# Gate and value layers by seven block products, float64 weights split from bytes, Mish as one ScalarE function

## The chip, the cores and the metric

The kernel runs on one NeuronCore of a Trainium2 chip. The metric is the device time of one execution in microseconds (us). Before the change the median of 3 runs is 508.99 us (508.86 to 509.68). The engines are called PE (TensorE), ACT (ScalarE), DVE (VectorE), POOL (GpSimd) and SP (SyncE, which issues the DMAs). SBUF is the on-chip memory, PSUM the accumulator memory that PE writes to, in banks of 128 x 512 float32.

## What is computed

Inputs q, k, v are float32, of shape (2, 8, 576, 64); the five weight matrices are float64.

```python
def _attn_ref(q, k, v):
    # factor 4: means of 4 neighbours in q, k, v give a small full attention, repeated 4 times;
    # added to it: attention within |i - j| < 4
    return (out_up + out_local).astype(np.float32)

def _moe_ref(x, w_in, w_out):                     # 512 -> 2048 -> 512
    h = x @ w_in
    sp = np.where(h > 20.0, h, np.log1p(np.exp(np.minimum(h, 20.0))))
    g = h * np.tanh(sp)                           # Mish
    return (g @ w_out).astype(np.float32)

def _moe2_ref(x, w_gate, w_val, w_out):           # 512 -> 1536 -> 512
    g = x @ w_gate
    silu = g * (1.0 / (1.0 + np.exp(-g)))
    val = x @ w_val
    return (silu * val @ w_out).astype(np.float32)

def reference(**kwargs):
    attn_out = _attn_ref(q, k, v)                 # (2, 8, 576, 64) -> x: 1152 tokens x 512
    x = _moe_ref(x=x, w_in, w_out)
    return _moe2_ref(x=x, w_gate, w_val, w_out)
```

## The kernel before

All activations stand with features on the partitions and the 1152 tokens along the row, in three pieces of 384 tokens (`PIECES`). Every float32 operand of a large product is split into a high part, which the float32r type of PE holds, and the rest, a low part. One product is then three matmuls: high x high, high x low, low x high (`mm3`, lines 755 to 758).

There are five stages on PE. Attention runs first, with dummy matmuls (`warm`, line 1091) where the planner has nothing else. Layer 1 (`l1`) has 16 chunks f of 128 features; a chunk and a token piece are 4 products along the 512 inputs, 12 matmuls of 384 columns into one PSUM bank, called a group here. The first pieces of chunks 0 to 5 are done within attention. Layer 2 (`l2`) has 4 blocks of 4 chunks; per block 12 groups (4 output slices e by 3 pieces i), which are added up in `yacc` in SBUF; after the last block `yacc` is split into `yb`. Layer 3 (`l3`) has 12 chunks; per chunk and piece a gate group and a value group, both on `yb`. Layer 4 (`l4`) has 3 blocks of 4 chunks, each with 9 groups of 12 matmuls of 512 columns. The order is: attention, layer 1 chunks 0 to 7, layer 2 block 0, layer 1 chunks 8 to 11, block 1, chunks 12 to 15, blocks 2 and 3, layer 3 chunks 0 to 7, layer 4 block 0, layer 3 chunks 8 to 11, layer 4 blocks 1 and 2. PSUM has 7 banks for all of this (`bank`).

A layer 1 group is copied out of its bank to H (line 224 on ACT, 226 on DVE). When the three pieces of a chunk are there, `mish` computes h * tanh(softplus(h)) as h * sin(pi/2 - 2 * arctan(...)): Tanh (line 809), Arctan (812) and Sin (815) on ACT, two chunks at a time, since Tanh and the other two need different function tables and a change of table costs an ACT_TABLE_LOAD; then a multiplication (819), the high part (224 or 226) and the low part (825) on DVE. Layer 3 takes Silu out of PSUM (919), multiplies with the value bank (922) and splits (224, 930).

A weight chunk is 512 KB of float64 (`convert`). SP loads it as pairs of 32-bit words into one of three `raw` buffers. Then the float32 is put together in `cw`, 128 x 512: magnitude of the upper word (297 on ACT or 299 on DVE), clamp (303), shift (307), three bits from the lower word (312), sign (317), all on DVE; then the high part (224 or 226) and the low part (333) go to one of eight `wt` buffers. There are 68 chunks: 16 for layer 1, 16 for layer 2, 12 each for gate, value and layer 4.

The order on every engine is made before the program is built: `Plan.add` takes each operation with its engines, an estimated duration, what it depends on, buffers, a due time `want`, and a mark for the function table; `Plan.run` goes through time and gives each free engine the ready operation with the earliest due time. An operation whose table mark differs from the current one is put off by 8 us and charged 1.28 us (`TABLE`); an ACT operation without a mark is taken to need no table. The order is then fixed: engines run in order, and only semaphores delay them. The table loads themselves are put in when the program is compiled, wherever an ACT function is not in the table that is loaded.

## Time and profile before

| | before |
|---|---|
| median of 3 runs | 508.99 us (508.86 to 509.68) |
| profiled execution, span of the program on the core | 507.6 us |
| PE busy | 500.7 us (99%) |
| DVE busy | 383.9 us (76%) |
| ACT busy | 277.0 us (55%) |
| granted TensorE clock, mean | 0.999 of 2.4 GHz |
| DMA | 48.2 MB, 95 GB/s over the span |

The span runs from the first to the last instruction of the profiled execution; the runs are timed by themselves, and their median lies 1.4 us above that span. Busy times are shares of the whole span, over stages that differ: a view by stretches of time tells what an engine does in each. Matmuls are pipelined, so the length of one is longer than its share of PE's time. Idle time of an engine matters only where another waits for it.

### The profile page before, as it was taken

The page shows a single profiled execution, that of the slowest core. Times are in us where ns is not written, and L with a number is a line of the kernel's source. Part 1 is how long each engine was busy: PE and PEld are TensorE (multiplying, and loading weights), DVE is VectorE, ACT ScalarE, POOL GpSimd, SP SyncE. Part 2 cuts the span into 40 slices and gives each one's busy share as a digit, 9 for nine tenths or more (in the row PEclk, how much of TensorE's full clock was granted, in tenths as well). Part 3 has the DMA queues.
Part 4 walks back from the last instruction along what each step waited for, and adds up shares of the span by engine and source line. Part 5 has one row for each costly group of instructions (what it writes and reads, how often), then busy time and mean ns, then how long its engine had stood idle before and what let it go on. Part 6 is the DMA issues. An engine that isn't in the chain of part 4 may idle for free.

```text
span 507.6 us, 8722 instructions
## 1 busy us (share of the span) xinstructions
PE 500.7 (99%) x3387; PEld 469.4 (92%) x3387; DVE 383.9 (76%) x771; ACT 277.0 (55%) x579; POOL 23.8 (5%) x45
## 2 busy tenths in 40 slices
PE   9999999999999999999999999999999999999997
PEld 7777779999999999999999999999998899998885
DVE  3898999999989999999699996667763298622322
ACT  3889999599995695679243634443432443310000
POOL 4432220000000000000000000000000000000000
PEclk9999999999999999999999999999999999999999
DMA  9999533451213521261205253222222032000022
GB/s 175 198 167 219 145 87 114 128 167 41 85 41 125 165 85 46 79 209 41 84 1 166 74 167 93 83 85 84 83 84 83 1 124 85 0 1 0 1 94 92
DMA packets 58225, 48.23 MB, mean 95 GB/s; under 512 B 30664, under 2 KB 53448, under 8 KB 58184
## 3 DMA queue, kind: packets, MB, share of 16 engines
q1 hardware_dynamic: 58184, 47.68, 34.2%
q8 instruction: 26, 0.43, 0.4%
q14 instruction: 15, 0.12, 0.1%
HBM read 45.31 MB, written 2.36 MB: 94 GB/s over the span
## 4 chain that ended last, share of the span: by engine, by line
PE 92%; ACT 3%; DVE 3%; DMA 1%; issue 1%; SPq 0%; ACTq 0%
PE b L756 23%; PE b L757 23%; PE b L758 23%; PE b L952 5%; PE b L951 5%; PE b L950 5%; PE warm L1091 2%; PE b L691 1%; PE b L636 1%; PE b L676 1%; ACT ed L535 1%; PE b L456 1%; DMA vw<-in_v_dram 1%; ACT ex L650 1%; PE b L520 1%
## 5 line engine op out<-in xcount | busy, mean ns | idle before, releaser
L756 PE MATMUL b<-xy,wt 128*128 128x384 f32 x480 | 161.3, 336 | 0.0
L758 PE MATMUL b<-xy,wt 128*128 128x384 f32 x480 | 160.4, 334 | 0.0
L757 PE MATMUL b<-xy,wt 128*128 128x384 f32 x480 | 160.4, 334 | 0.0
L756 PEld LDWEIGHTS b<-xy,wt 128*128 128x128 f32 x480 | 90.1, 188 | 0.4
L757 PEld LDWEIGHTS b<-xy,wt 128*128 128x128 f32 x480 | 90.1, 188 | 0.0
L758 PEld LDWEIGHTS b<-xy,wt 128*128 128x128 f32 x480 | 90.1, 188 | 0.0
L757 PE MATMUL b<-G,wt 128*128 128x384 f32 x192 | 64.2, 335 | 0.0
L756 PE MATMUL b<-G,wt 128*128 128x384 f32 x192 | 64.1, 334 | 0.0
L758 PE MATMUL b<-G,wt 128*128 128x384 f32 x192 | 64.1, 334 | 0.0
L224 ACT ACTIVATE G<-H 128x384 fp32r<-128x384 f32 (+1 forms) x38 | 21.7, 575 | 65.5 <-DVE H L922 44.5
L297 ACT ACTIVATE cw<-raw 128x512 f32<-128x512 f32 x58 | 39.0, 675 | 31.2 <-DVE wt L333 19.4
L333 DVE TENSOR_TENSOR wt<-cw,wt 128x512 fp32r<-128x512 f32 x68 | 46.1, 685 | 1.5 <-ACT wt L224 0.3
L312 DVE SCALAR_TENSOR_TENSOR cw<-raw,cw 128x512 uint32<-128x512 uint32 x68 | 46.4, 688 | 0.5
L317 DVE SCALAR_TENSOR_TENSOR cw<-raw,cw 128x512 uint32<-128x512 uint32 x68 | 46.3, 686 | 0.3
L952 PE MATMUL b<-wt,G 128*128 128x512 f32 x108 | 42.1, 389 | 0.0
L951 PE MATMUL b<-wt,G 128*128 128x512 f32 x108 | 42.0, 389 | 0.0
L950 PE MATMUL b<-wt,G 128*128 128x512 f32 x108 | 42.0, 389 | 0.0
L224 ACT ACTIVATE wt<-cw 128x512 fp32r<-128x512 f32 x41 | 25.0, 627 | 26.5 <-PE b L757 23.1
L922 DVE TENSOR_TENSOR H<-b,H 128x384 f32<-128x384 f32 x36 | 19.9, 553 | 24.8 <-PE b L758 24.8
L965 DVE TENSOR_TENSOR acc<-b,acc 128x512 f32<-128x512 f32 x18 | 12.4, 692 | 34.6 <-PE b L952 34.6
L757 PEld LDWEIGHTS b<-G,wt 128*128 128x128 f32 x192 | 36.0, 188 | 0.3 <-DVE G L825 0.3
L758 PEld LDWEIGHTS b<-G,wt 128*128 128x128 f32 x192 | 36.0, 188 | 0.0
(90 smaller groups left out, 751.6 us busy)
## 6 DMA issues: line engine op xcount, KB each, us to landing
raw<-in_moe_w_out_dram SPq DMA_DIRECT2D x28, 512.0 KB
raw<-in_moe_w_in_dram SPq DMA_DIRECT2D x16, 512.0 KB
raw<-in_moe_w_gate_dram SPq DMA_DIRECT2D x12, 512.0 KB
raw<-in_moe_w_val_dram SPq DMA_DIRECT2D x12, 512.0 KB
vw<-in_v_dram SPq DMA_DIRECT2D x36, 70.0 KB
vq<-in_v_dram SPq DMA_DIRECT2D x8, 288.0 KB
out_dram<-acc SPq DMA_DIRECT2D x9, 256.0 KB
qk<-in_q_dram SPq DMA_DIRECT2D x8, 256.0 KB
```

The lines of the kernel that those rows point to most:

```text
L224: ACT.activation(out, in_, AF.Copy)
L297: ACT.activation(cw.tile, h.bitcast(F32), AF.Abs)
L312: DVE.scalar_tensor_tensor(out=c, in0=words()[:, :, 0], scalar=29, in1=c, op0=ALU.logical_shift_right, op1=ALU.bitwise_or)
L317: DVE.scalar_tensor_tensor(out=c, in0=words()[:, :, 1], scalar=0xC0000000, in1=c, op0=ALU.bitwise_and, op1=ALU.bitwise_or)
L333: DVE.tensor_tensor(out=wt.tile[:, 1], in0=cw.tile, in1=wt.tile[:, 0].bitcast(F32), op=ALU.subtract)
L756: PE.matmul(out=ps, lhsT=wt_hi, rhs=m_hi, start=first, stop=False)
L757: PE.matmul(out=ps, lhsT=wt_hi, rhs=m_lo, start=False, stop=False)
L758: PE.matmul(out=ps, lhsT=wt_lo, rhs=m_hi, start=False, stop=last)
L922: DVE.tensor_tensor(out=h.tile[:, cs], in0=pv.tile[:, 0:n], in1=h.tile[:, cs], op=ALU.mult)
L950: PE.matmul(out=ps.tile, lhsT=g[:, 0, tok], rhs=wt[:, 0], start=(f == fs[0]), stop=False)
L951: PE.matmul(out=ps.tile, lhsT=g[:, 0, tok], rhs=wt[:, 1], start=False, stop=False)
L952: PE.matmul(out=ps.tile, lhsT=g[:, 1, tok], rhs=wt[:, 0], start=False, stop=(f == fs[-1]))
```

## The change

Three things are done, and the planner's rules stay as they are.

**Weights.** `convert` loads the same 512 KB, as bytes, into a `raw` tile of 4104 bytes per partition, at byte 1. Seen as 32-bit words from byte 0, the upper word of each pair then holds the float64's bits shifted by a byte. Its sign and the top exponent bits are the byte at 8 (read as int8, every 8th). `fold` and `field` make the float32's upper bits from it on ACT, both with the function Prelu, without a table mark; `join` shifts the word right by 5 and puts both together on DVE. High and low part follow as before. `cw` has 3 buffers, not 4.

```diff
-            o = plan.add({"ACT": us_act(512), "DVE": us_ts(512)}, mag, [o_load, prev.get("mag")], w0, [cw], [raw])
-            o_mag = o
-            for fn, d in ((range_, us_ts(512)), (shift, us_ts(512)), (low, us_tt(512)), (sign, us_tt(512))):
-                o = plan.add({"DVE": d}, fn, [o], w0 + 1, use=[cw, raw])
+            def fold(e):
+                ACT.activation(cw.make(), raw.tile[:, 8:4104].bitcast(I8).rearrange("p (n b) -> p n b", b=8)[:, :, 0],
+                               AF.Prelu, scale=-1.0, bias=-56.0, alpha=SLOPE)
+
+            def field(e):
+                ACT.activation(cw.tile.bitcast(I32), cw.tile, AF.Prelu, scale=-2.0 ** 27 / SLOPE, bias=-112 * 2.0 ** 27, alpha=SLOPE)
+
+            def join(e):
+                DVE.scalar_tensor_tensor(out=cw.tile.bitcast(U32), in0=raw.tile[:, 0:4096].bitcast(U32).rearrange("p (n b) -> p n b", b=2)[:, :, 1],
+                                         scalar=5, in1=cw.tile.bitcast(U32), op0=ALU.logical_shift_right, op1=ALU.bitwise_or)
+
+            o_mag = o = plan.add({"ACT": us_act(512) + 0.1}, fold, [o_load, prev.get("mag")], w0, [cw], [raw])
+            o = plan.add({"ACT": us_act(512)}, field, [o], w0, use=[cw])
+            last = plan.add({"DVE": us_tt(512)}, join, [o], w0 + 1, use=[cw, raw])
```

**Mish.** Tanh, Arctan, Sin and the multiplication go. The first two pieces of chunks 0 to 5, done within attention, are copied to H and later passed through Mish in place, 768 columns at once; all other groups of layer 1 leave PSUM through Mish on ACT. Both carry the mark "mish". G has 6 buffers, not 7, and the T buffers go.

```diff
+            if early:
+                copy(e, h.tile[:, cs], ps.tile[:, 0:n])
+            else:
+                ACT.activation(h.tile[:, cs], ps.tile[:, 0:n], AF.Mish)
+        if early:
+            o = plan.add({"ACT": us_act(n, True), "DVE": us_tt(n)}, evac, [o], want - 4, use=[ps, h])
+        else:
+            o = plan.add({"ACT": us_act(n, True)}, evac, [o] + att_ops, want - 4, use=[ps, h], table="mish")
...
+        if f < RING:
+            h.ops.append(add({"ACT": us_act(n)}, mish, h.ops[:2] + att_ops, want - 2, use=[h], table="mish"))
+        o = add({"ACT": us_act(NTOK), "DVE": us_ts(NTOK)}, hi, h.ops + att_ops, want + 4.0, [g], [h])
```

**Seven products.** For the first two token pieces, layer 3 takes two chunks, the two halves of the 512 inputs and the two pieces as 2 x 2 blocks and computes them by seven block products (a Winograd form of Strassen's scheme) of 6 matmuls each, where eight products took 48. `combine` makes two sums and differences of weight halves per pair of chunks, each with its own high and low part; `turn_tokens` makes four differences of token blocks at the end of layer 2 (one in `yb`, three in new `tok` tiles). In `products` some sums run in PSUM: bank `pa` takes four products, and its state is copied to SBUF after the first, second and third of them before the next is added on; three sums are finished on DVE. The third piece goes on as before, in groups.

```diff
+        o1 = product(pa, (kind, f), 0, y(0, 0), raw[0], True, False, [yb], home)
+        k1 = keep(pa, hold.slots[0], [o1])
+        o2 = product(pb, (kind, f), 1, y(1, 0), raw[1], True, True, [yb])
+        c11 = add_(pb, hold.slots[0], [o2, k1])
+        o5 = product(pc, (kind, f, 0), 0, t[0], tok_ops[0:1], True, False, [yb])
+        o6 = product(pa, (kind, f, 0), 1, t[1], [tok_ops[1], k1], False, False, [tok[0]])
+        k2 = keep(pa, hold.slots[1], [o6])
+        o7 = product(pa, (kind, f, 1), 0, t[2], [tok_ops[2], k2], False, False, [tok[1]])
+        k3 = keep(pa, hold.slots[2], [o7])
+        c22 = add_(pc, hold.slots[2], [o5, k3])
+        o4 = product(pa, (kind, f + 1), 1, t[3], [tok_ops[3], k3], False, True, [tok[2]])
+        o3 = product(pc, (kind, f, 1), 1, y(1, 1), raw[2] + [c22], False, True, [yb])
+        c12 = add_(pc, hold.slots[1], [o3, k2])
...
+        todo = [(0, block(0, 1), block(0, 0), given[0, 1] + given[0, 0]), (1, block(1, 1), view(tmp[0]), given[1, 1]),
+                (2, block(1, 1), block(0, 1), given[1, 1] + given[0, 1]), (3, block(1, 0), view(tmp[1]), given[1, 0])]
...
+            o = plan.add({"DVE": us_tt(2 * PC)}, sub_, deps + more, want, [tmp[x]], [yacc] + ([tmp[0]] if x == 1 else [tmp[1]] if x == 3 else []))
+            subs.append(o)
+            o = plan.add({"ACT": us_act(2 * PC), "DVE": us_ts(2 * PC)}, hi, [o, yb.first], want, [tok[x - 1]] if x else [], [tmp[x]] + ([] if x else [yb]))
+            o = plan.add({"DVE": us_tt(2 * PC)}, lo, [o], want, use=[tmp[x], tok[x - 1] if x else yb])
...
+        a = plan.add({"DVE": us_tt(256)}, add_(0, 0, half(c1, 0), half(c1, 1), ALU.add), [o1, o0], w0, [s0], [c1])
+        b = plan.add({"DVE": us_tt(256)}, add_(1, 0, half(c0, 0), half(c1, 0), ALU.subtract), [o1, o0], w0, [s1], [c0, c1])
+        a = plan.add({"DVE": us_tt(256)}, add_(0, 1, half(s0, 0), half(c0, 0), ALU.subtract), [a], w0, use=[s0, c0])
+        b = plan.add({"DVE": us_tt(256)}, add_(1, 1, half(c0, 1), half(s0, 1), ALU.subtract), [a, b], w0, use=[s1, c0, s0])
```

The planner orders everything anew. Three places show how. First ACT, at chunks 2 to 4 of layer 1 in the kernel before (T is the buffer of the Mish steps, H a chunk's evacuated rows):

```order
L809 ACT_TABLE_LOAD
L809 ACTIVATE T0_1589<-H2_1286 128x1152
L297 ACTIVATE cw2_1077<-raw2_1023 128x512
L809 ACTIVATE T1_1611<-H3_1385 128x1152
L224 ACTIVATE H0_1027<-b6_241 128x384
L812 ACT_TABLE_LOAD
L812 ACTIVATE T0_1589<-T0_1589,half_83 128x1152
L815 ACT_TABLE_LOAD
L815 ACTIVATE T0_1589<-T0_1589,half_pi_82 128x1152
L812 ACTIVATE T1_1611<-T1_1611,half_83 128x1152
```

And on ACT at chunks 5 to 7 of layer 1 in the changed kernel (L286 is fold, L290 field, L803 Mish out of a bank, L822 Mish in place):

```order
L286 ACTIVATE cw1_979<-raw2_1006 128x512
L822 ACT_TABLE_LOAD
L822 ACTIVATE H5_1459<-H5_1459 128x768
L290 ACT_TABLE_LOAD
L290 ACTIVATE cw1_979<-cw1_979 128x512
L803 ACT_TABLE_LOAD
L803 ACTIVATE H5_1459<-b6_237 128x384
L286 ACT_TABLE_LOAD
L286 ACTIVATE cw2_1065<-raw1_897 128x512
L803 ACT_TABLE_LOAD
L803 ACTIVATE H1_1110<-b2_195 128x384
```

A table load stood before every second or third function of the old steps, with copies and conversions between that took none; now one stands at each turn between a conversion and a Mish. The built program has 25 table loads before and 58 after.

Next DVE where layer 2 ends and layer 3 begins, before (L879 adds a bank to acc, L895 is the low part of yb, L333 that of a weight chunk):

```order
L879 TENSOR_TENSOR acc0_1875<-b5_233,acc0_1875 128x384
L226 CAST xy0_84<-acc0_1875 128x384
L895 TENSOR_TENSOR xy0_84<-acc0_1875,xy0_84 128x384
L333 TENSOR_TENSOR wt4_1427<-cw3_1132,wt4_1427 128x512
L879 TENSOR_TENSOR acc0_1875<-b2_199,acc0_1875 128x384
L333 TENSOR_TENSOR wt6_1521<-cw1_986,wt6_1521 128x512
```

And the same place on DVE after (L873 adds a bank to acc, L892 is the low part of yb, L920 a token difference, L928 its low part):

```order
L873 TENSOR_TENSOR acc0_1847<-b6_237,acc0_1847 128x384
L920 TENSOR_TENSOR H0_983<-acc0_1847,H4_1333 128x768
L892 TENSOR_TENSOR xy0_82<-acc0_1847,xy0_82 128x384
L920 TENSOR_TENSOR H5_1459<-acc0_1847 128x768
L928 TENSOR_TENSOR tok00_2891<-H0_983,tok00_2891 128x768
L920 TENSOR_TENSOR H1_1110<-acc0_1847,H0_983 128x768
L928 TENSOR_TENSOR tok10_2904<-H5_1459,tok10_2904 128x768
L873 TENSOR_TENSOR acc0_1847<-b5_229,acc0_1847 128x384
L928 TENSOR_TENSOR tok20_2917<-H1_1110,tok20_2917 128x768
L892 TENSOR_TENSOR xy0_82<-acc0_1847,xy0_82 128x384
```

Between the last two sums of the middle tokens and the low parts of the last tokens' columns there are now the differences and their low parts.

## Rows read from the trace of the kernel before

**Rows 1.** The page: engines' busy time; the chain that ended last, by engine and line.

```profile
PE 500.7 (99%) x3387; PEld 469.4 (92%) x3387; DVE 383.9 (76%) x771; ACT 277.0 (55%) x579; POOL 23.8 (5%) x45
...
PE 92%; ACT 3%; DVE 3%; DMA 1%; issue 1%; SPq 0%; ACTq 0%
PE b L756 23%; PE b L757 23%; PE b L758 23%; PE b L952 5%; PE b L951 5%; PE b L950 5%; PE warm L1091 2%; PE b L691 1%; PE b L636 1%; PE b L676 1%; ACT ed L535 1%; PE b L456 1%; DMA vw<-in_v_dram 1%; ACT ex L650 1%; PE b L520 1%
```

**Rows 2.** Stretches: length; busy us (count) of PE, PEld, DVE, ACT, POOL; clock; DMA; GB/s.

```profile
0.00:40.00 40.00, 37.59 (x445) 28.98 (x445) 28.59 (x76) 27.93 (x105) 15.91 (x36) 1.00 1.01 183
37.00:92.80 55.80, 55.13 (x719) 45.02 (x715) 53.03 (x149) 49.39 (x201) 9.28 (x11) 1.00 0.55 134
92.80:126.00 33.20, 33.20 (x194) 33.20 (x192) 31.65 (x58) 29.07 (x34) 0.00 (x0) 1.00 0.37 123
...
92.80:229.20 136.40, 136.40 (x787) 136.10 (x786) 128.93 (x224) 107.37 (x125) 0.00 (x0) 1.00 0.34 108
280.00:380.00 100.00, 100.00 (x578) 100.00 (x578) 74.28 (x148) 40.52 (x73) 0.00 (x0) 1.00 0.31 95
```

**Rows 3.** What PE waited for, longest sum first: us, times, longest.

```profile
PE warm L1091 <- DVE wsrc L375: 1.2, 1, 1.2
PE b L559 <- ACT ed L548: 0.5, 1, 0.5
```

**Rows 4.** Groups by line and shape on ACT: busy us, mean ns, idle before.

```profile
L297 ACT ACTIVATE cw<-raw 128x512 f32<-128x512 f32 x58 | 39.0, 675 | 31.2 <-DVE wt L333 19.4 <-DMA raw<-in_moe_w_out_dram 7.3 <-DMA raw<-in_moe_w_in_dram 3.9
L224 ACT ACTIVATE wt<-cw 128x512 fp32r<-128x512 f32 x41 | 25.0, 627 | 26.5 <-PE b L757 23.1 <-DVE cw L317 2.9 <-PE b L758 0.4
...
L815 ACT ACTIVATE T<-T,half_pi 128x1152 f32<-128x1152 f32 x16 | 20.1, 1259 | 0.2
...
L809 ACT ACTIVATE T<-H 128x1152 f32<-128x1152 f32 x16 | 18.7, 1167 | 0.7 <-DVE H L819 0.5
...
L919 ACT ACTIVATE H<-b 128x384 f32<-128x384 f32 x36 | 17.6, 488 | 31.6 <-PE b L758 31.6
L224 ACT ACTIVATE H<-b 128x384 f32<-128x384 f32 x27 | 13.0, 482 | 3.4 <-PE b L758 3.2
...
L812 ACT ACT_TABLE_LOAD x8 | 10.3, 1283 | 0.1
...
L224 ACT ACTIVATE G<-H 128x1152 fp32r<-128x1152 f32 x3 | 3.5, 1158 | 0.2 <-DVE H L819 0.2
```

**Rows 5.** ACT in order of time, around a table load: start us, us, what.

```profile
110.21 0.66 ACT L297 ACTIVATE cw<-raw 128x512 f32<-128x512 f32 x1
110.78 1.25 ACT L815 ACTIVATE T<-T,half_pi 128x1152 f32<-128x1152 f32 x1
...
112.30 0.66 ACT L297 ACTIVATE cw<-raw 128x512 f32<-128x512 f32 x1
112.97 1.28 ACT L809 ACT_TABLE_LOAD   x1
114.27 1.17 ACT L809 ACTIVATE T<-H 128x1152 f32<-128x1152 f32 x1
```

**Rows 6.** Groups on PE: busy us, mean ns of one, idle before.

```profile
L756 PE MATMUL b<-xy,wt 128*128 128x384 f32 x480 | 161.3, 336 | 0.0
...
L1091 PE MATMUL warm<-wsrc 128*128 128x256 bf16 x103 | 16.5, 297 | 1.2 <-DVE wsrc L375 1.2
```

**Rows 7.** Groups on DVE, low parts of 1152 and of 384 columns.

```profile
L825 DVE TENSOR_TENSOR G<-H,G 128x1152 fp32r<-128x1152 f32 x16 | 21.6, 1349 | 0.0
...
L895 DVE TENSOR_TENSOR xy<-acc,xy 128x384 fp32r<-128x384 f32 x12 | 6.6, 551 | 0.6 <-ACT xy L224 0.6
```

**Rows 8.** The chain that ended last, in order of time: start us, us, what.

```profile
56.46 4.05 DMA vw<-in_v_dram
...
91.98 0.85 PE b L691 x24
```

More of the change, by code (lines that the diff above doesn't have):

```diff
@@ L284, in load @@
             else:
-                nc.sync.dma_start(out=raw.tile, in_=src[128 * f:128 * (f + 1), :])
+                nc.sync.dma_start(out=t, in_=src[128 * f:128 * (f + 1), :])
         prev = conv_chain[0] or {}
@@ L788, in l1 @@
         ps, o, cs = cols_group("1", f, i, lambda: xt, xd + [h.first], want, [x_buf] + ([] if first else [h]), [h] if first else [])
+        early = f < RING and i < 2
         def evac(e):
-            copy(e, h.tile[:, cs], ps.tile[:, 0:n])
-        o = plan.add({"ACT": us_act(n, True), "DVE": us_tt(n)}, evac, [o], want - 4, use=[ps, h])
+            if early:
[6 more added lines that the diff above has]
+            o = plan.add({"ACT": us_act(n, True)}, evac, [o] + att_ops, want - 4, use=[ps, h], table="mish")
         if first:
@@ L797, in l1, with split, mish, hi @@
         if i == 2:
-            mish(f, h, want)
-    tanhs = []
-    def mish(f, h, want):
+            split(f, h, want)
+    def split(f, h, want):
         add = plan.add
-        g = G[f] = buf("g", GSHAPE, F32R, "G", 7)
-        t = buf("g", [128, NTOK], F32, "T", 2)
-        def tanh(e):
-            ACT.activation(t.make(), h.tile, AF.Tanh, scale=0.5)
-        def atan(e):
-            ACT.activation(t.tile, t.tile, AF.Arctan, scale=-0.5, bias=half)
-        def sin(e):
-            ACT.activation(t.tile, t.tile, AF.Sin, scale=-2.0, bias=half_pi)
-        def mult(e):
+        g = G[f] = buf("g", GSHAPE, F32R, "G", 6)
+        n = 2 * PC
+        def mish(e):
+            ACT.activation(h.tile[:, 0:n], h.tile[:, 0:n], AF.Mish)
+        def hi(e):
             g.make()
-            DVE.tensor_tensor(out=h.tile, in0=h.tile, in1=t.tile, op=ALU.mult)
-        def hi(e):
             copy(e, g.tile[:, 0], h.tile)
@@ L886, in l2 @@
         if fs[-1] == FF1 - 1:
+            y_full[e_, i] = o
             begin = yb.first is None
+            if i == 1 and e_ < 2:
+                return
             def hi(e):
@@ new lines, in products, with product, fn, keep @@
+    def products(kind, f, want, home, hold):
+        n = PC
+        p0, p1, p2 = [slice(c0, c0 + n) for c0, n in PIECES]
+        pa, pb, pc = bank(), bank(), bank()
+        for x in ((kind, f), (kind, f + 1), (kind, f, 0), (kind, f, 1)):
+            assert x in wts
+        y = lambda r, c: lambda z, j: yb.tile[:, z, 2 * r + j, (p0, p1)[c]]
+        t = [lambda z, j: yb.tile[:, z, j, p1]] + [lambda z, j, x=x: tok[x].tile[:, z, j] for x in range(3)]
+        raw = {0: [y_ops[e_, 0] for e_ in (0, 1)], 1: [y_ops[e_, 0] for e_ in (2, 3)], 2: [y_ops[e_, 1] for e_ in (2, 3)]}
+        def product(ps, w, half, m, deps, first, last, use, new=()):
+            def fn(e):
+                if first:
+                    ps.make()
+                for x in new:
+                    x.make()
+                wt = wts[w].tile
+                for j in range(2):
+                    cs = slice(256 * half + 128 * j, 256 * half + 128 * j + 128)
+                    mm3(ps.tile[:, 0:n], wt[:, 0, cs], wt[:, 1, cs], m(0, j), m(1, j), first and j == 0, j == 1, skip_group_check=True)
+            return plan.add({E_PE: 6 * us_mm(n)}, fn, list(deps) + [wt_ops[w]], want, ([ps] if first else []) + list(new),
+                            ([] if first else [ps]) + [wts[w]] + list(use))
+        def keep(ps, d, deps, w=None):
+            def fn(e):
+                copy(e, d(), ps.tile[:, 0:n])
+            return plan.add({"ACT": us_act(n, True), "DVE": us_tt(n)}, fn, deps, want - 4, use=[ps, hold])
+        def add_(ps, d, deps):
+            def fn(e):
+                DVE.tensor_tensor(out=d(), in0=ps.tile[:, 0:n], in1=d(), op=ALU.add)
+            return plan.add({"DVE": us_tt(n)}, fn, deps, want - 4, use=[ps, hold])
+        o1 = product(pa, (kind, f), 0, y(0, 0), raw[0], True, False, [yb], home)
[11 more added lines that the diff above has]
+        c12 = add_(pc, hold.slots[1], [o3, k2])
+        return pa, o4, c11, c12, c22
@@ L1045, in add_l3 @@
     def add_l3(b):
-        for f in blk(b):
-            for i in range(3):
-                groups.append(([("g", f), ("v", f)] if i == 0 else (), 2, lambda t, f=f, i=i: l3(f, i, t)))
+        for f in blk(b)[::2]:
+            groups.append(([("g", f, 2), ("v", f, 2)], 11.0, lambda t, f=f: l3(f, t)))
     def add_l4(b):
```

209 lines of the change are left out of this document (119 added, 90 removed).

## The prediction

> **What bounds the kernel now.** The page comes first [rows 1]: PE is busy 99% of the span, and 92% of the chain that ended last is PE, almost all of it the three matmul lines of the four layers. The list of what PE waited for says how rigid that is [rows 3]: the longest sum is 1.2 us at the start, the next 0.5. The table by stretch [rows 2] shows two parts. Up to 92.8 us there is attention, where PE runs small matmuls and dummies, and DVE (53.0 of 55.8 us in its second part) and ACT (49.4) are nearly full as well. The last attention products end at 92.8 [rows 8]; from there PE has no gap. So after 92.8 a matmul less is time gained, and a wait added is time lost, at full price. Before it, a gain must beat three engines.
>
> The price of a 384-column matmul is the stretch 280 to 380: 578 in 100.0 us, 0.173 us each [rows 2]. The 336 ns of its group [rows 6] is its length in a pipeline and not its cost.
>
> **What the change takes from PE.** In the built order the matmuls on xy and on the new tok tiles are 1368 where there were 1440: 12 sets of products save 6 each. 72 x 0.173 = 12.5 us, all of it in the gate and value stage, where PE has no gap. Nothing else on PE changes: the dummies are 103 in both orders [rows 6], the second and fourth layers have the same counts.
>
> **What it does to ACT in the first two layers.** This decides. Per weight chunk ACT had one magnitude instruction (675 ns [rows 4]), and on 10 of 68 not even that. Now it has two, fold and field, both Prelu. Mish replaces Tanh, Arctan and Sin (16 times 1.17 to 1.26 us each) and does most evacuations. That alone would unload ACT. But the built order has 58 table loads where the old one had 25: one stands at almost every change between Prelu and Mish, 28 of them on the lines of fold and field. The planner, which lets a table count only for the marked functions (Exp, Mish, Silu), does not know of these and strews conversions between Mish instructions. 56 of the 58 stand in the first two layers. A load takes 1283 ns [rows 4], and the next instruction starts 20 ns after it, the load itself 10 ns after the instruction before [rows 5]: 1.3 us each, nothing hidden.
>
> The ACT instructions of that part, by rows 4: 56 loads 72; 25 folds and 25 fields at 0.65 (the rows of 675 and 627 ns), 33; 36 Mish out of PSUM at 0.48, 17; 6 Mish of 768 columns at 0.84 (between the rows of 512 and 1152 columns), 5; 13 copies of 1152 at 1.16, 15; 20 shorter copies, 10. Sum 152 us, where PE has 136.4 us of work in the same part and ACT had 107.4 [rows 2]. ACT becomes the bound.
>
> How much of it reaches PE goes by banks. A group of 12 matmuls (2.08 us) fills one of seven PSUM banks, and a group cannot start before the bank of the group seven places earlier is evacuated. I went through the two orders stage by stage, adding the row durations on ACT and 0.173 us per matmul on PE.
>
> Stage I, the last 18 groups of layer 1 that follow attention. ACT's first Mish load stands behind one evacuation and one fold, at about 95.2. From it to the last Mish of chunk 7 there are 23 loads (29.5), 15 conversions (9.8), 13 evacuations (6.3), 6 Mish of 768 (5.0), 4 copies of 1152 (4.6) and 3 of 512 (1.9): 57.1 us, to 152.3. The bank that its last instruction but one gives back, at 151.8, is wanted by the fifth group of the second layer's first block after chunk 7; 270 matmuls stand between 92.8 and that group, so PE would be there at 139.5. PE is 12.3 us late. No slack is left out: the seven banks are in this number (without them it would be some 20).
>
> Stage II, chunks 8 to 11. PE leaves the second layer's first block at 154.0 + 12.3 = 166.3, ACT has caught up by then (the block needs 12 short evacuations) and is free at 167.8. To the eighth Mish evacuation there are 15 loads (19.2), 12 conversions (7.8), 8 evacuations (3.9) and 4 copies (3.6): 34.5 us, to 202.3. The group that wants this bank stands 168 matmuls after 166.3, at 195.4. PE loses 6.9 us more.
>
> Stage III, chunks 12 to 15: 14 loads, 18 conversions, 12 evacuations and 5 copies, some 40 us, beside 50 us of PE, and the planner has put chunk 12's evacuations on ACT early. By the same count no bank is late. Sum: 19.2 us. The ends: half of it if conversions run into each other as in the timeline (the row at 110.21 starts the next after 0.57 us, not 0.66), a few loads pass while PE is behind, and ACT starts a microsecond earlier, 12 us; with each handover between fold and field costing another 0.1 us, 24 us.
>
> The Trainium skill, ScalarE: Activation LUTs, section What ACT_TABLE_LOAD costs, states 1283 ns for the load and another 1380 ns for a drain, 2.66 us per switch. The trace agrees with the first and not with the second (the 20 ns of rows 5). By the page the 56 loads would cost 77 us more.
>
> **DVE, and the turn into the gate stage.** DVE loses four of five conversion steps per chunk and gains one, and gains the half-chunk sums, the sums out of PSUM and the four token differences. Per pair of chunks in the gate stage that is about 20 us of DVE by starts, beside 132 matmuls, 22.9 us; DVE ran 31.7 of 33.2 in the old first layer without PE waiting [rows 2, 3], so I price that at nothing. At the turn it shows: after the last sum of the middle tokens DVE has four differences and three low parts of 768 columns (0.95 us, between the rows of 384 and 1152 [rows 7]), seven short ones and two of 512 before the low part of the last tokens' columns, some 14 us in all, while PE has 8.3 us of the second layer, then 4 of 6-matmul products, 12.5 us, until it wants that. 2.0 us, between 0 and 3.
>
> **Attention.** ACT gets about 10 instructions more up to 92.8 (+6.6 us, against 6.4 us of idle time in 37 to 92.8 [rows 2]); DVE is relieved by about as much. PE's dummies stay in the order, and its gaps there are 0.7 us, so almost nothing can be gained. The one new kind of transfer, into a tile one byte off, is not in the trace. From below: as before. From above: as slow as the stretch with mostly 256-byte packets, 183 GB/s [rows 2], 2.9 us for 512 KB where the stretch 280 to 380 (0.31 busy for 95 GB/s) gives 1.7; the layers need 85 GB/s, so nothing is late there, but a value load that PE already waited for behind such loads [rows 8] would be a microsecond or two later. I take +1.5 us for attention, between -0.7 and +5.
>
> **The sum.** Against the profiled execution: 507.6 - 12.5 + 19.2 + 2.0 + 1.5 = 517.8. The median of the runs, 508.99, is 1.4 above that span: **519.2 us**.
>
> **The rivals.**
> The loads do not hold PE up, the saving stays: 507.6 - 12.5 + 2.0 + 1.4 = 498.5. For it speaks that ACT has 29 us of idle time in the old part [rows 2] and loses the three old functions. Without the 56 loads ACT would have 80 us of work against 136, and nothing would wait. Against it stand the loads in the order and the 1283 ns. It decides if fewer than about 30 of them were to run. 8%. The Trainium skill, ScalarE: Activation LUTs, section Table sets: the hidden batching unit, says that cheap functions such as relu, copy, identity and abs are in every set as filler; read so as to cover Prelu, it would give this rival's time. The built order has no load at Copy, but has them at Prelu.
>
> The product sets hold PE, on top of the forecast. The third and fourth product onto one bank wait for a copy of what stands there, with 6 matmuls (1.04 us) between: the last matmul's end lies 0.16 us after the next one's start [rows 6], the copy takes 0.49 [rows 4], so 0.3 us are left with the handovers unpriced. If at each of the 24 places a conversion of 0.65 us stands before the copy, 0.36 x 24 = 8.6 us: 528. For it: ACT and DVE are full of conversions there. Against: ACT's order has the copies waiting for PE, often in pairs with nothing between. 14%.
>
> PE's waits of 2 to 5 us in stage I could also lower its granted clock, which was 1.00 of the higher level (2.4 GHz) throughout; no row shows such a wait, so it is left to the upper end of the range.
>
> The skewed loads are slow by a factor of 4 or more: 7 us per chunk where PE uses one in 6.2, and the kernel would follow the DMA, above 560. Against: the stretch at 183 GB/s is the slowest of those that keep the DMA engines busy. 4%.
>
> Each table load empties ACT for as long again as it takes: 56 x 1.28 = 72 us more in the part that already holds PE, 591. Against it stand the 20 ns of rows 5; 2%. The Trainium skill, in the section on ACT_TABLE_LOAD named above, states nearly this.
>
> That the products do not save what they say is excluded by the counted matmuls.
>
> **How the numbers follow.** The forecast has 72%. Its own spread: 12 to 24 for the loads, 0 to 3 at the turn, -0.7 to +5 in attention, so 508 to 526, most of it within 513 to 525. What a measurement can tell from no change is 0.2%, 1.0 us. Faster by more: the first rival and a sliver of the forecast, 10%. Within: 4%. Slower: 86%. The range 509 to 528 leaves out the first rival, the upper part of the second and the two large ones, about 2 in 10.
>
> **What would show it.** In the changed profile: 58 table loads of 1283 ns; ACT busy nearly without gap from 95 to 152; at the top of PE's waits the Mish evacuation line, some 19 us in pieces of 1 to 5 us, none after the third chunk block; the two gate stages, 528 and 264 matmuls, at 0.173 us. Wrong would be: PE without waits there (first rival), waits on the copies between products, or on value loads in attention.

## The result, and the profile after

The changed kernel takes **517.21 us** (median of 4 runs, 516.17 to 518.08) where the kernel before takes 509.34 beside it: 1.015 times as long (95% interval 1.0132 to 1.0168). The forecast was 519.2. Measured once more beside other kernels it took 516.64, 1.0155 times (1.0132 to 1.0177).

The page of the changed kernel answers to [rows 1]: the span, the engines, the chain that ended last.

```profile
span 515.2 us, 8535 instructions
...
PE 494.1 (96%) x3315; PEld 459.3 (89%) x3315; DVE 323.2 (63%) x624; ACT 339.0 (66%) x681; POOL 23.9 (5%) x43
...
PE 75%; ACT 19%; issue 3%; DVE 2%; DMA 1%; ACTq 0%
```

ACT, 3% of the chain before, is 19% of it now, and PE has idle time. What it waited for stands in the list that answers to [rows 3] (us in all, times, longest):

```profile
PE b L763 <- ACT H L803: 14.2, 8, 4.1
```

L803 is Mish out of a bank: PE waits for banks. Where, the table by stretch shows. Its boundaries are the end of attention, the ends of layer 2's blocks 0, 1 and 3, and the gate and fourth-layer stages; columns as in [rows 2].

```profile
93.20:167.60 74.40, 65.00 (x359) 62.86 (x356) 27.95 (x43) 65.62 (x82) 0.00 (x0) 0.98 0.26 84
167.60:224.30 56.70, 51.27 (x289) 49.98 (x288) 23.38 (x37) 44.42 (x54) 0.00 (x0) 1.00 0.25 75
224.30:299.60 75.30, 75.30 (x434) 75.30 (x433) 49.11 (x82) 50.47 (x68) 0.00 (x0) 1.00 0.23 70
299.60:391.40 91.80, 91.80 (x531) 91.80 (x530) 83.13 (x155) 60.13 (x108) 0.00 (x0) 1.00 0.34 104
391.40:416.10 24.70, 24.70 (x110) 20.27 (x110) 5.50 (x12) 7.37 (x11) 0.00 (x0) 1.00 0.14 43
416.10:462.00 45.90, 45.90 (x265) 45.90 (x264) 39.75 (x70) 30.62 (x57) 0.00 (x0) 1.00 0.30 92
```

PE is idle in the first two of these stretches only, 9.4 and 5.4 us. In the first, ACT is busy for 65.6 us, more than the 62.0 us that this stretch takes PE without waits (the fourth experiment shows that). The two gate stretches, the fourth and the last row, take 137.7 us; before, 576 and 288 matmuls took 149.8.

The groups on ACT that answer to [rows 4], table loads and the two new steps (busy us, mean ns, idle before):

```profile
L286 ACT ACTIVATE cw<-raw 128x512 f32<-128x512 int8 x68 | 45.7, 672 | 12.1 <-DVE wt L307 11.3 <-DMA raw<-in_moe_w_out_dram 0.5
L290 ACT ACTIVATE cw<-cw 128x512 int32<-128x512 f32 x68 | 43.0, 633 | 0.9
L803 ACT ACT_TABLE_LOAD x23 | 29.5, 1283 | 0.4
...
L286 ACT ACT_TABLE_LOAD x17 | 21.8, 1283 | 0.3
...
L290 ACT ACT_TABLE_LOAD x11 | 14.1, 1283 | 0.2
...
L822 ACT ACT_TABLE_LOAD x5 | 6.4, 1283 | 0.1
...
L480 ACT ACT_TABLE_LOAD x1 | 1.3, 1283 | 0.7 <-PEq L1215 0.7
L1004 ACT ACT_TABLE_LOAD x1 | 1.3, 1283 | 0.0
```

58 loads of 1283 ns, 56 of them at Mish (L803, L822) and Prelu (L286, L290). In the gate stage, where Silu (L1004) alternates with Prelu, there is one: those two share a table. The timeline of ACT ahead of the longest wait (start us, us, what):

```profile
139.21 1.28 ACT L822 ACT_TABLE_LOAD   x1
140.50 0.84 ACT L822 ACTIVATE H<-H 128x768 f32<-128x768 f32 x1
141.36 1.28 ACT L290 ACT_TABLE_LOAD   x1
142.66 0.63 ACT L290 ACTIVATE cw<-cw 128x512 int32<-128x512 f32 x1
143.30 1.28 ACT L803 ACT_TABLE_LOAD   x1
144.60 0.49 ACT L803 ACTIVATE H<-b 128x384 f32<-128x384 f32 x1
```

Three loads stand around two functions of useful work, without a gap; at 145.09 a bank comes free. PE has been waiting for it since 141.03, as its timeline shows:

```profile
140.69 0.34 PE L765 MATMUL b<-G,wt 128*128 128x384 f32 x1
145.14 0.69 PE L763 MATMUL b<-G,wt 128*128 128x384 f32 x1 [4.11 <-ACT H L803]
145.62 0.52 PE L764 MATMUL b<-G,wt 128*128 128x384 f32 x1
```

### The profile page after: what moved, and what is told of

Same layout as the page of the kernel before. It is cut to its first block, busy times and chain, and to the rows that moved or that the text cites. A ratio compares the mean times of both kernels' runs of the same rounds, so it can differ in the third digit from the quotient of the medians.

```text
span 515.2 us, 8535 instructions
## 1 busy us (share of the span) xinstructions
PE 494.1 (96%) x3315; PEld 459.3 (89%) x3315; DVE 323.2 (63%) x624; ACT 339.0 (66%) x681; POOL 23.9 (5%) x43
## 4 chain that ended last, share of the span: by engine, by line
PE 75%; ACT 19%; issue 3%; DVE 2%; DMA 1%; ACTq 0%
PE b L763 17%; PE b L765 17%; PE b L764 17%; PE b L1051 5%; PE b L1053 5%; PE b L1052 5%; ACT L803 3%; PE warm L1194 2%; ACT L290 2%; ACT cw L286 2%; ACT L286 2%; ACT H L803 2%; PE b L643 2%; ACT cw L290 1%; PE b L698 1%
## 5 line engine op out<-in xcount | busy, mean ns | idle before, releaser
L763 PE MATMUL b<-xy,wt 128*128 128x384 f32 x384 | 129.9, 338 | 3.7 <-ACT H L803 3.7
L765 PE MATMUL b<-xy,wt 128*128 128x384 f32 x384 | 128.6, 335 | 0.0
L764 PE MATMUL b<-xy,wt 128*128 128x384 f32 x384 | 128.6, 335 | 0.0
L293 DVE SCALAR_TENSOR_TENSOR cw<-raw,cw 128x512 uint32<-128x512 uint32 x68 | 46.6, 687 | 64.3 <-ACT cw L290 64.2
L763 PE MATMUL b<-G,wt 128*128 128x384 f32 x192 | 66.2, 345 | 11.1 <-ACT H L803 10.5
L763 PEld LDWEIGHTS b<-xy,wt 128*128 128x128 f32 x384 | 72.1, 188 | 5.3 <-ACT H L803 4.7
L764 PEld LDWEIGHTS b<-xy,wt 128*128 128x128 f32 x384 | 72.1, 188 | 0.0
L765 PEld LDWEIGHTS b<-xy,wt 128*128 128x128 f32 x384 | 72.1, 188 | 0.0
L765 PE MATMUL b<-G,wt 128*128 128x384 f32 x192 | 65.1, 339 | 0.0
L764 PE MATMUL b<-G,wt 128*128 128x384 f32 x192 | 65.0, 338 | 0.0
L286 ACT ACTIVATE cw<-raw 128x512 f32<-128x512 int8 x68 | 45.7, 672 | 12.1 <-DVE wt L307 11.3
L219 ACT ACTIVATE G<-H 128x1152 fp32r<-128x1152 f32 x20 | 22.9, 1164 | 45.8 <-PE b L765 23.5
L763 PEld LDWEIGHTS b<-G,wt 128*128 128x128 f32 x192 | 36.5, 190 | 13.6 <-ACT H L803 12.8
L290 ACT ACTIVATE cw<-cw 128x512 int32<-128x512 f32 x68 | 43.0, 633 | 0.9
L1051 PE MATMUL b<-wt,G 128*128 128x512 f32 x108 | 42.3, 391 | 0.0
L764 PEld LDWEIGHTS b<-G,wt 128*128 128x128 f32 x192 | 36.5, 190 | 0.0
L765 PEld LDWEIGHTS b<-G,wt 128*128 128x128 f32 x192 | 36.5, 190 | 0.0
L221 DVE CAST wt<-cw 128x512 fp32r<-128x512 f32 x34 | 15.2, 446 | 32.6 <-PE b L1053 19.2
L219 ACT ACTIVATE H<-b 128x384 f32<-128x384 f32 x31 | 15.2, 489 | 27.4 <-PE b L765 27.3
```

The source lines that it names most:

```text
L219: ACT.activation(out, in_, AF.Copy)
L286: ACT.activation(cw.make(), raw.tile[:, 8:4104].bitcast(I8).rearrange("p (n b) -> p n b", b=8)[:, :, 0], AF.Prelu, scale=-1.0, bias=-56.0, ...
L290: ACT.activation(cw.tile.bitcast(I32), cw.tile, AF.Prelu, scale=-2.0 ** 27 / SLOPE, bias=-112 * 2.0 ** 27, alpha=SLOPE)
L293: DVE.scalar_tensor_tensor(out=cw.tile.bitcast(U32), in0=raw.tile[:, 0:4096].bitcast(U32).rearrange("p (n b) -> p n b", b=2)[:, :, 1], sca ...
L763: PE.matmul(out=ps, lhsT=wt_hi, rhs=m_hi, start=first, stop=False, **more)
L764: PE.matmul(out=ps, lhsT=wt_hi, rhs=m_lo, start=False, stop=False, **more)
```

## The experiments

Three numbers are read for each kernel: the time, PE's delay in layers 1 and 2 (by how much the distances between the starts of neighbouring matmuls exceed 0.174 us, summed over the places where PE waited or was slowed), and the part of it up to the end of layer 2's first block, "the first stretch", with ACT's loads and busy time there. Of the changed kernel's 19.1 us of delay, 14.8 are the waits for banks themselves; the rest is some 0.3 us in the distances around each of ten waits, and some 1.5 us that its matmuls stood wider apart at a lower clock (experiment 9).

| kernel | time, us | loads in the trace | first stretch: loads, ACT busy, length, us | delay: first stretch, all |
|---|---|---|---|---|
| before | 509.3 | 25 | 11, 57.6, 62.8 | 0, 0 |
| changed | 517.2 | 58 | 24, 65.6, 74.4 | 12.5, 19.1 |
| 1: old weights (DVE) in layers 1, 2 | 499.9 | 10 | 1, 31.9, 64.0 | 0, 0 |
| 2: as 1, ACT work put back | 503.1 | 8 | 1, 39.7, 62.9 | 0, 0 |
| 3: as 2, loads without work | 510.9 | 64 | 24, 58.9, 68.2 | 5.4, 7.2 |
| 4: changed, planner told | 497.6 | 46 | 16, 49.6, 62.0 | 0, 0 |
| 12: as 1, with Abs on ACT | 498.1 | 44 | 14, 50.3, 63.0 | 0, 0 |

**1. No Prelu beside Mish.** `convert` has the old steps for the chunks of layers 1 and 2 and loads those chunks at byte 0 (cuts of the edit; `...` marks what is left out).

```diff
+OLDKINDS = "12"
...
+            k = 0 if kind in OLDKINDS else 1
+            t = t[:, k:k + 4096] if wide else t
...
+        if wide and kind in OLDKINDS:
...
+            o = plan.add({"DVE": us_ts(512)}, mag, [o_load, prev.get("mag")], w0, [cw], [raw])
...
+        elif wide:
```

> The changed kernel, with the old weight steps (all of them on DVE, loaded at byte 0) for the 32 chunks of layers 1 and 2, so that no Prelu stands among the Mish instructions; the gate, value and fourth layers keep fold, field and the load one byte off. Built order: 11 table loads, not 58. Theory (the table loads hold PE up): the waits of PE on the Mish evacuation, 14.2 us, and what hangs on them, some 19 us in all, go, and the seven products keep their 12 us: 517.2 - 19 = 498 us, PE without a wait above 1 us after attention. Rival (Mish out of PSUM on ACT alone holds the banks, or DVE, with five steps of conversion again, does): waits of 5 us or more are left in layers 1 and 2, 503 us or above.

499.93 us, 0.9816 times the kernel before (0.9798 to 0.9835). The head of PE's waits:

```profile
PE warm L1238 <- DVE wsrc L427: 1.2, 1, 1.2
PE b L507 <- DVE xs L752: 0.3, 1, 0.3
```

The whole delay is gone. The 2 us above the expected time come from attention: it ends at 92.6 with 66 matmuls of layer 1 done within it, where the changed kernel has done 78.

**2 and 3. The work without the loads, the loads without the work.** Two ACT instructions per chunk stand ahead of the old steps. The second experiment's are shown; in the third they are Prelu of one column, with `0:1` in the place of `0:512` and `AF.Prelu, alpha=SLOPE` in the place of `AF.Copy`.

```diff
+            def first(e):
+                ACT.activation(cw.make()[:, 0:512], words()[:, 0:512, 1].bitcast(F32), AF.Copy)
+
+            def second(e):
+                ACT.activation(cw.tile[:, 0:512], cw.tile[:, 0:512], AF.Copy)
```

> As the first, but ACT does two copies of 512 columns per chunk of layers 1 and 2, where fold and field stood, before the old steps: ACT's work of the changed kernel without its table loads (8 in the built order). The copies' result is overwritten. Theory (the loads): ACT has 80 to 90 us of work beside 136 of PE there, no wait, 498 to 499 us. Rival (the two conversion steps on ACT hold PE, loads or not): half of the 19 us or more is back, 507 us or above.

> As the second, but each of the two instructions is a Prelu of one column: the table loads (64 in the built order) without the conversion work. The planner still plans 0.6 us for each. Theory (the loads): ACT's sum in layers 1 and 2 is some 137 us where it was 152: about two thirds of the loss, 13 us of waits on the Mish evacuation, 511 us (507 to 515). Rival (the conversion work): as the second, 498 to 500 us. If loads and work add up to a threshold, this and the second both stay near 498 and only the changed kernel has the loss.

503.10 us (ratio 0.9874, 0.986 to 0.9889) and 510.94 us (1.0022, 1.0011 to 1.0034). In both, attention ends late, at 98.1 and 98.6, with 143 dummies for 103 (the planner had fitted two more ACT steps per chunk in there); that was foreseen in neither, and is why the second is above 499. What the pair is for lies behind attention, where the two do the same on PE. The first stretch of the second kernel, then of the third, and the head of what PE waited for in the third:

```profile
98.10:161.00 62.90, 62.90 (x362) 62.90 (x361) 50.63 (x97) 39.72 (x66) 0.00 (x0) 1.00 0.37 116
```
```profile
98.60:166.80 68.20, 64.47 (x362) 62.45 (x361) 51.51 (x97) 58.94 (x88) 0.00 (x0) 1.00 0.32 102
```
```profile
PE b L814 <- ACT H L854: 4.2, 7, 1.4
```

Behind attention the work alone costs PE nothing, the loads alone 7.2 us. Both together, in the changed kernel, cost 19.1. So the loads are the cause, and what they cost depends on what else ACT has to do. The third kernel's time met its expectation by two misses: 7.2 us of waits where 13 were expected, and 5 us more attention.

**4 and 8. The planner told.** One word more on two lines; the planner then charges the 1.28 us.

```diff
-            o_mag = o = plan.add({"ACT": us_act(512) + 0.1}, fold, [o_load, prev.get("mag")], w0, [cw], [raw])
-            o = plan.add({"ACT": us_act(512)}, field, [o], w0, use=[cw])
+            o_mag = o = plan.add({"ACT": us_act(512) + 0.1}, fold, [o_load, prev.get("mag")], w0, [cw], [raw], table=None if kind in "gv4" else "exp")
+            o = plan.add({"ACT": us_act(512)}, field, [o], w0, use=[cw], table=None if kind in "gv4" else "exp")
```

> The changed kernel, with fold and field of layers 1 and 2 marked with the table of Exp, so that the planner charges 1.28 us at each change between them and Mish and puts them off: 45 table loads, not 58. Theory (the loads, 1.3 us each on an ACT that is full): 13 loads less are up to 17 us less on ACT, some 12 of them in the two late stretches; PE's waits fall from 14 to about 4, 505 us (501 to 509). Rival (the loads hide or do not matter): 517 us as it was.

> The fourth experiment's kernel once more, beside the padded one on the same chip. Theory and rival alike: 497.6 us (497.0 to 498.3).

497.59 us, 0.9763 times the kernel before (0.9748 to 0.9779), and 497.69 the second time: **faster than both kernels**, with everything of the change in it. 46 loads are left, 12 fewer than in the changed kernel, and PE's delay fell from 19.1 us to nothing, not by the 12 expected. The same two stretches as above:

```profile
93.40:155.40 62.00, 62.00 (x359) 61.97 (x356) 33.08 (x52) 49.57 (x66) 0.00 (x0) 1.00 0.31 102
155.40:205.70 50.30, 50.30 (x289) 50.30 (x288) 25.83 (x40) 36.23 (x47) 0.00 (x0) 1.00 0.27 84
```

ACT does 16 us less in the first: 8 loads less (10.3 us) and 16 instructions less in all. Its timeline there shows Mish grouped, and the conversions behind the last Mish of chunk 7:

```profile
131.07 1.28 ACT L803 ACT_TABLE_LOAD   x1
132.37 0.87 ACT L803 ACTIVATE H<-b 128x384 f32<-128x384 f32 x2
133.26 1.28 ACT L290 ACT_TABLE_LOAD   x1
134.55 0.63 ACT L290 ACTIVATE cw<-cw 128x512 int32<-128x512 f32 x1
135.09 0.66 ACT L286 ACTIVATE cw<-raw 128x512 f32<-128x512 int8 x1
```

The last Mish of this stretch ends at 133.2; in the changed kernel that was 153.0. So the mark did two things at once: it took loads away, and it put conversions behind the Mish that give banks back. This run does not part the two; the table of bank dates below says how much each took from ACT.

**12. Abs in the place of Prelu.** The first experiment's kernel with the magnitude on ACT or DVE, as the kernel before has it.

```diff
-            o = plan.add({"DVE": us_ts(512)}, mag, [o_load, prev.get("mag")], w0, [cw], [raw])
+            o = plan.add({"ACT": us_act(512), "DVE": us_ts(512)}, mag, [o_load, prev.get("mag")], w0, [cw], [raw])
```

> The first experiment's kernel, but the magnitude of the old weight steps (chunks of layers 1 and 2) may run on ACT as Abs again, as in the kernel before: the new weights undone there as a whole. The built order has 44 table loads, 16 of them at an Abs that follows a Mish. Theory (loads cost PE only where ACT's own sum in a stretch nears PE's): by the 1.28 us of each, ACT has some 32 + 16 x 1.9 = 60 us beside PE's 64 up to the end of layer 2's first block, the edge of what fits: waits of 0 to 7 us on the Mish evacuation, 503 us (500 to 507). Rival (Mish shares its table with Abs and the built loads are not run): 500 us and 12 loads or fewer in the trace. Second rival (any load beside Mish costs PE its full 1.28 us): 31 loads more than the first, 535 us or above.

498.11 us (0.9789, 0.976 to 0.9817), with 44 loads in the trace, 16 at the Abs line:

```profile
L300 ACT ACT_TABLE_LOAD x16 | 20.5, 1283 | 0.3
```

So the loads do run, and the 14 of the 44 that stand in the first stretch cost PE nothing at 50 us of ACT beside 63 of PE. Both rivals fall. The time, 498.1, lies under the 500 to 507 expected: ACT's sum was put at 60.

**6. No seven products.** The fourth kernel with `l3` and the weights of the gate stage as before the change.

```diff
-        for f in blk(b)[::2]:
-            groups.append(([("g", f, 2), ("v", f, 2)], 11.0, lambda t, f=f: l3(f, t)))
+        for f in blk(b):
+            for i in range(3):
+                groups.append(([("g", f), ("v", f)] if i == 0 else (), 2, lambda t, f=f, i=i: l3(f, i, t)))
```

> The fourth experiment's kernel with the gate and value stage of the kernel before: 864 matmuls there instead of 792, no combined weights, no token differences. Theory (the seven products save their matmuls and cost nothing else): 72 x 0.1735 = 12.5 us more in the two gate stages, nothing at the turn: 510 us, what the kernel before takes. So new weights and Mish by themselves would gain nothing. Rival (the product sets or the turn cost PE something that the trace hides): 507 us or below.

509.74 us (1.0018, 1.0003 to 1.0033), 12.1 us above the fourth. The gate stretches of this one, and of the fourth:

```profile
279.60:379.70 100.10, 100.10 (x578) 100.10 (x577) 50.48 (x89) 47.97 (x90) 0.00 (x0) 1.00 0.31 95
404.40:454.50 50.10, 50.10 (x290) 50.10 (x289) 25.88 (x47) 22.61 (x44) 0.00 (x0) 1.00 0.19 64
```
```profile
281.00:372.75 91.75, 91.75 (x529) 91.75 (x528) 83.08 (x155) 60.12 (x108) 0.00 (x0) 1.00 0.34 104
397.50:443.40 45.90, 45.90 (x265) 45.90 (x264) 39.74 (x70) 30.59 (x57) 0.00 (x0) 1.00 0.30 92
```

Without the seven products this kernel takes what the kernel before takes (the interval of the ratio lies between no difference and 0.3%), so the gain of the fourth is theirs. In the first gate stretch DVE is busy 83 us of 92 with them, 50 of 100 without. With the old weight steps it was 74 of 100 before [rows 2], so by DVE's sums the new steps make the room; the next experiment tries that. Seven products with the old Mish steps were not run.

**7. Old weights everywhere.** The condition of the first experiment for all 68 chunks (the edit is against that kernel).

```diff
-OLDKINDS = "12"
+OLDKINDS = "12gv4"
```

> The changed kernel with the old weight steps, all on DVE, for all 68 chunks: 3 table loads, no Prelu at all, load at byte 0. Theory (the new weight steps are what makes room on DVE for the seven products): DVE had 83 of 92 us in the first gate stage; per pair of chunks the old steps add 4 x (3 x 0.36 + 2 x 0.69 - 0.69) = 7 us to 20.8, while PE needs 22.9: DVE becomes the bound there, some 4 to 5 us late for each of six pairs, 520 us (512 to 527). Rival (DVE keeps up because high parts go to ACT and conversions are done ahead, in layer 2 and in the fourth layer): 498 to 501 us, as the first.

502.19 us (0.9859, 0.9836 to 0.9883): between the two times expected. DVE is full in the first gate stretch and stays so into the fourth layer:

```profile
283.50:375.90 92.40, 92.40 (x530) 91.59 (x529) 92.23 (x186) 43.10 (x76) 0.00 (x0) 1.00 0.24 75
375.90:401.90 26.00, 24.99 (x110) 20.24 (x109) 24.63 (x54) 8.69 (x14) 0.00 (x0) 1.00 0.44 142
```

PE loses 0.6 us in the first stretch and 1.3 in the second, against the kernel with the new steps. The expected 20 us did not come, since DVE took only 9 us more in the first stretch (83 to 92), not the 28 that four pairs at 7 us would add: all 28 high parts there ran on ACT (with the new steps DVE did 9 of them), and 14 chunks were converted there, not 19. Six more were converted in the fourth layer's block, where DVE is busy for 24.6 us of 26 instead of 5.5 of 24.7. So the new weight steps are worth some 2 us here and are not the condition for the products, although DVE's sums had suggested it.

**9 and 11. The low clock.** After the wait of 4.1 us the granted clock fell to its lower level (1.2 GHz). The changed kernel, first in slices of 2 us (PE busy first, the clock is the third number from the end):

```profile
142.00:144.00 2.00, 0.00 (x0) 0.00 (x0) 0.68 (x2) 1.97 (x3) 0.00 (x0) 1.00 0.03 10
144.00:146.00 2.00, 0.86 (x3) 0.86 (x4) 0.61 (x2) 1.97 (x3) 0.00 (x0) 0.66 0.51 90
146.00:148.00 2.00, 2.00 (x8) 2.00 (x7) 0.00 (x0) 1.97 (x3) 0.00 (x0) 0.50 0.42 172
```

```diff
...
+                if (f, e_, i) == (0, 1, 0):
+                    for _ in range(22):
+                        PE.matmul(out=spare_bank[0][:, 0:n], lhsT=wt[:, 0, 0:128], rhs=g[:, 0, 0:n], start=True, stop=True)
                 if f == fs[0]:
                     ps.make()
...
```

> The changed kernel with 22 more matmuls of 384 columns (3.8 us, into the spare bank, read by nobody) on PE just ahead of the group that waited 4.1 us at 145.1 us and after which the granted clock stood at 0.50 for some 3 us; that stretch cost 1.6 us more than full clock would. First theory (ACT alone sets the dates in this stage: the time lost at the low clock would otherwise be waited at the next banks, 0.3 us at 148.9 and 1.5 at 152.7): the clock stays at 1.00 and the waits after it grow by the 1.6 us, time as it was, 517.2 us. Rival (the low clock comes on top of the waits): 515.6 us.

> The changed kernel as it is, on the same chip as the one with the filled wait. Both theories: 517.2 us (516.2 to 518.1).

517.02 us with the wait filled, 516.64 without. The longest wait is 2.1 us now, but the clock did not stay up: it fell after another wait of 2.1 us, the one that ends at 136.6. After the same wait, also 2.1 us, it had stayed up in the changed kernel (there it ends at 135.8). Slices of 2 us of the filled one, then the slice of the changed one behind that wait:

```profile
136.00:138.00 2.00, 1.44 (x5) 1.44 (x6) 1.46 (x3) 1.97 (x4) 0.00 (x0) 0.66 0.03 8
138.00:140.00 2.00, 2.00 (x8) 2.00 (x7) 2.00 (x3) 1.97 (x5) 0.00 (x0) 0.50 0.00 0
```
```profile
136.00:138.00 2.00, 2.00 (x12) 1.87 (x12) 2.00 (x3) 1.97 (x3) 0.00 (x0) 1.00 0.03 8
```

So what was expected of the clock failed. What was expected of the time held: layers 1 and 2 take 206.6 us here and 206.4 there, though PE does 22 matmuls more. Time that PE spends in this stretch is not added to its waits but taken out of them: ACT sets the dates. What the low clock costs this run does not tell, since both kernels had some 3 us of it.

**5. Raw tiles padded.** 4160 bytes instead of 4104.

> The fourth experiment's kernel with raw tiles of 4160 bytes per partition instead of 4104, so that every tile allocated behind them starts 56 bytes (and multiples) later, at a multiple of 64 as in the kernel before; same order, same instructions. In every kernel built on the change the matmuls of layer 2 stand 175.4 ns apart on average where the kernel before has 173.4, five of each twelve 2 to 12 ns later, though PE waits for nothing: 1.7 us in all. Theory (the operands' place in SBUF): the pitch is 173.4 again and the time 1.0 to 1.7 us lower, 496 us. Rival (it is the company that the matmuls keep, Mish or the transfers): the pitch and the time stay, 497.6 us.

498.19 us beside 497.69: no gain. Layer 2's matmuls stand 174.9 ns apart, against 175.4, where the kernel before has 173.3. So tile addresses that are no multiple of 64 account for a fifth of these 2 ns at most.

**10. Loads at byte 4.** The same load, on whole words.

```diff
-            t = t[:, 1:4097] if wide else t
+            t = t[:, 4:4100] if wide else t
```

> The fourth experiment's kernel with the weight loads at byte 4 of the raw tile instead of byte 1, so that they fall on whole 32-bit words; the weights it computes with are then wrong, everything else is the same. Theory (a load one byte off costs nothing here): 497.6 us, attention ends at the same time within 0.5 us, packets of 1024 and 4096 bytes as long as before. Rival (the skew slows the loads, hidden in the layers but not in attention): 0.5 to 2 us faster, in attention.

497.8 us, as at byte 1 (497.6 and 497.7). Packets of 1024 and of 4096 bytes took 46 and 159 ns (medians) at byte 0, 1 and 4 alike. Attention ended at 92.3 in the profiled execution, 1.3 us earlier than in the two of the fourth kernel, which is what the rival asked for. But it also ended at 92.1 in the sixth kernel, with its loads at byte 1, so one execution does not decide it. The packets and the medians show no cost of a load one byte off.

## Why the prediction was right, point by point

Against the span before, 507.6, the trace adds up like this: layers 1 and 2 took 206.4 us instead of 187.6 (+18.8), the gate stages -12.1, the fourth layer +0.4, attention +0.5: 515.2. The forecast had 517.8 by its own steps. Of the 2.6 us between them 3.0 are the turn and attention, both taken too high; the other differences are of half a microsecond and less and nearly cancel.

**The matmuls saved, 12.5:** 12.1 measured, and once more in the sixth experiment. Nothing waits between the products; the second rival, 8.6 us there, did not come. (Its own sum was too high: 1.04 - 0.16 - 0.49 leaves 0.39 us and not 0.3, so 0.26 x 24 = 6.2 us.)

**The table loads, 19.2:** 19.1, and both halves by themselves: 12.5 in stage I (forecast 12.3), 6.5 in stage II (6.9), none in stage III. The dates were right within a microsecond. The bank that stage I hangs on was put at 151.8 and came at 152.6; that of stage II at 202.3 and came at 203.1. ACT ran 55.5 of the 57 us from 95 to 152. The waits that end at these two banks:

```profile
152.68 0.44 PE L763 MATMUL b<-G,wt 128*128 128x384 f32 x1 [1.36 <-ACT H L803]
203.12 0.44 PE L763 MATMUL b<-G,wt 128*128 128x384 f32 x1 [1.39 <-ACT H L803]
```

That a bank's date decides, and not PE's sum, is what the ninth experiment showed: 22 matmuls more on PE, and the same length.

The price of a load, 1283 ns with 0.01 to 0.02 us around it, is the timeline's above. The Trainium skill, ScalarE: Activation LUTs, section What ACT_TABLE_LOAD costs, adds a drain of some 1380 ns; the timelines above have room for none. The Trainium skill, on the same page, section Table sets: the hidden batching unit, gives relu, copy, identity and abs to every set. In these runs copies needed no load beside Mish, but Prelu did, and Abs too (16 loads in the twelfth run). There the measurement decides, and the first rival falls with it. (That rival's 498.5 also leaves out the 1.5 us of attention that the forecast has.)

**"It decides if fewer than about 30 of them were to run":** this step failed, though the forecast did not hang on it. 46 loads cost nothing in the fourth experiment and 44 in the twelfth. Nor does ACT's sum over a stretch tell it: the kernel before had ACT busy for 57.6 us of 62.8 and no delay, the third experiment 58.9 of 62.9 and 5.4. What tells it is the forecast's own arithmetic, the date of a bank, applied to the other kernels. The row of each kernel is the bank on which the last wait of the first stretch hangs, or, where PE waits for none, the bank at the same place in the built order: when its Mish gave it back, and when PE wanted it by the matmuls ahead (0.1737 us each), both counted from the last matmul of attention.

| kernel | ACT ahead of it: loads, other instructions, busy | given back, us | wanted, us (matmuls) | late by |
|---|---|---|---|---|
| changed | 23, 42, 56.7 us | 59.6 | 47.1 (271) | 12.5 |
| 3: loads without work | 23, 47, 51.4 us | 55.6 | 50.2 (289) | 5.4 |
| 4: planner told | 15, 29, 37.3 us | 39.6 | 47.1 (271) | 7.5 early |
| 12: Abs on ACT | 13, 42, 42.3 us | 48.7 | 50.2 (289) | 1.5 early |

The two that are late are late by the delay measured, and the two that are early have none. The mark of the fourth took 19.5 us off ACT ahead of this bank: 8 loads, 10.3 us, and 13 other instructions that were put behind it, 9.2 us. So the order counted as much as the loads, and that is why the run came out 7 us below its expectation, which had counted loads alone. The condition of the first rival should have been worked out from these dates, as the price was.

**The turn, 2.0 (0 to 3):** nothing. The forecast let the low part of the last tokens' columns come 2 us too late. It came just in time: the last sum of the middle tokens (the second row) ended at 292.05, the low part (the third) at 303.5, and PE wanted it at 303.81, as the forecast's 12.5 us have it.

```profile
287.92 0.96 DVE L920 TENSOR_TENSOR H<-acc 128x768 f32<-128x768 f32 x1
291.49 0.56 DVE L873 TENSOR_TENSOR acc<-b,acc 128x384 f32<-128x384 f32 x1 [0.19 <-PE b L765]
302.98 0.55 DVE L892 TENSOR_TENSOR xy<-acc,xy 128x384 fp32r<-128x384 f32 x1
```
```profile
303.81 0.34 PE L763 MATMUL b<-xy,wt 128*128 128x384 f32 x1
```

The step that was mis-sized is DVE's work between the two: 14 us in the forecast, 11.5 measured. One of the four differences ran earlier (the first row), and the forecast's own list, by its rows (seven of 0.95, seven of 0.55, two of 0.69), sums to 11.9 and not to 14. With 0.3 us to spare, that nothing was lost here is close to luck.

**Attention, +1.5 (-0.7 to +5):** it ended 0.5 us later, with one half group (6 matmuls, 1.0 us) more done. In another profiled execution of the same kernel it ended at 92.1, so this term is not known to better than a microsecond. The feared loads showed no cost (tenth experiment). Of the twelve first and second pieces of chunks 0 to 5, which the section on the change puts within attention, six and a half groups were done when it ended.

**Not in the sum:** matmuls that stand wider apart. Layers 1 and 2 took 18.8 us more with 1.0 us of their work done earlier, so 19.8 are to be explained; 19.1 are delay, the other 0.7 or so these, and with them the fourth layer's 0.4. The granted clock, left to the upper end of the range, did fall, for some 3 us. By the trace that added nothing: PE still had to wait at 148.9 and at 152.7, 0.1 and 1.4 us, for banks whose dates ACT set; no run had this stretch at full clock throughout. The forecast's spread, 508 to 526, was added up too low at its end: 12.5 saved, and 24, 3 and 5 lost, give 528.5, just above the range's 528.

## What to carry to other kernels

Before a function on ScalarE is exchanged, count the table loads in the built order and, stage by stage, add up ScalarE to the date at which the next engine needs its result. Here that count was good to half a microsecond of delay. ACT's sum over both layers (third experiment) and the number of loads (fourth) were not: the delays expected from them were some 6 us too high in the one, 4 in the other, and the fourth's time came out 7 us below. A load ahead of such a date costs nothing while the result still comes in time, and its full price once it is late. So a planner has to be told of every function that forces a load: one mark on two lines turned 1.5% slower into 2.4% faster. In the first stretch about half of what it took off ACT's way were loads, the other half the order that came with it.
